# Retention scores of a fused three-layer kernel: three float32r products replaced by plain float32 products with two heads in the halves of the array's rows

## The chip, the cores and the metric

The kernel runs on one core of one Trainium2 chip. The metric is device time in microseconds for one launch; lower is better. Three runs of the kernel before gave 1452.89, 1457.00 and 1457.19 us, a median of 1457.0 us.

## The reference

Three layers follow one another. The first is retention over 8 batches, 8 heads, 576 positions and 64 features a head: scores, a causal decay mask, and a product with v. Its output, 4608 rows of 512, goes through a mixture of 8 experts with one expert for each row, and then through a dense layer with a squared rectifier.

```
scores = scale * np.matmul(q, k.transpose(0, 1, 3, 2))
ret = scores * Dmat[None, :, :, :]
attn = np.matmul(ret, v)                     # 8 x 8 x 576 x 64
logits = x @ w_gate;  expert_idx = np.argmax(logits, axis=1)
xe = x[mask];  h = np.maximum(xe @ w1[e], 0.0);  ye = h @ w2[e]
out[mask] = gate_w[mask, None] * ye          # for each of 8 experts
h = x @ w_in;  r = np.maximum(h, 0.0);  out = (r * r) @ w_out
```

## The kernel before

The work runs in three stages, one after the other: retention with the routing of the rows to experts, the experts, and the dense layer. The change touches only the first.

The 4608 rows are 36 tiles of 128. A tile's input, `in`, is 1 MB: q and k with their features on the partitions, v and k with their tokens on the partitions. In the array of partitions of q and k, partitions 0 to 63 hold one head of a pair and 64 to 127 the other, so that four blocks of 128 columns hold the eight heads. Five buffers hold `in`.

A loop over t, written out by hand in `body`, sets the order of work on each engine; each engine takes its instructions in that order. In round t it does the following.

- SyncE's queue starts the load of tile t+4 (L291), which needs the buffer of tile t-1, and then writes the rows of tile t-1 to DRAM in four transfers (L406).
- `scores(t + 1)`: TensorE multiplies k by q into two PSUM tiles `sc`, out of a ring of three. VectorE multiplies each by the mask into `r` (L343).
- `scale_v(t + 2)`: GpSimd scales v into `vs` (L316).
- `out_x(t)`: TensorE multiplies q by the running state (L385; for every ninth tile, which holds the ends of two batches, L378 with `zq`, a copy of q with zeros), and adds the product of `r` and `vs` (L389). VectorE scales the sum into `x` (L397) and transposes it in blocks into `xr` (L399).
- `state(t)`: TensorE adds k times v to the state (L361), and ScalarE copies it out into `sts` (L368).
- On every second tile there are router logits (L417, L421, L426, L427), and between t = 11 and the end one routing step at the end of a round, mostly on VectorE (L449 to L508, L162 to L191).
- In rounds 14, 20, 26 and 32 the first expert's weights are split into two float32r parts, by ScalarE (L99) and VectorE (L100).

A float32 product can be had from float32r products by splitting each operand into a high part, rounded to float32r, and the rest. `split(t + 3)` does that for k and q: ScalarE rounds k into `kh` (L299) and the two halves of q into `qh` (L302); GpSimd subtracts to get `kl` (L303), and VectorE and GpSimd subtract to get the two halves of `ql` (L306; one half each when t > 6, both on VectorE before). The tiles `qh` and `ql` (`qb` in the trace) hold each pair of heads side by side in 256 columns, with zeros in the other head's partitions, so one product over all 128 partitions gives the scores of two heads. `scores` then takes three such products for each pair: high by high, high by low, low by high (L338 to L340), 12 matmuls of 256 columns for a tile. The first two tiles, t < `EASY`, skip the split and use plain float32 operands straight from `in`, one head in partitions 0 to 63 and one in 64 to 127 (L330), 8 matmuls of 128 columns for a tile; each stands as two matmul records in the trace.

For t up to 6, `split(t + 3)` stands after `state(t)`; later it stands before `out_x(t)`.

Of the kernel before, what the change touches and what calls it, by code (L numbers as in the profile page):

```python
# [27 lines left out]
EASY = 2  # L28
BUSY = 6
# [10 lines left out]
def body(ctx, tc, att, tab_v, tab_x, masks, wg, ident, pick, cst, wu, wd, out):  # L40
# [70 lines left out]
    # ---- float64 weights: sign, exponent and 20 bits of the mantissa come from the high word, the  # L111
    # other 32 bits from the low word; kept in DRAM as two float32r parts ----
# [44 lines left out]
    def route(rt, t0, t1, ri, bank, inv, ct):  # L157
        """Adds, for the tokens of tiles t0 to t1 whose place among their expert's is ri, their numbers at their
        slots: the slot within a tile picks the row, expert and tile pick the column."""
# [58 lines left out]
    # a row of x_d and y_d keeps its features in the order (32-row quadrant, 128-feature chunk, 32)  # L218
    x_q = x_d.rearrange("n (a c) -> (n a) c", a=4)

    # (expert 0 has its first matrix's rows in that order too, so its rows need no reordering)
# [26 lines left out]
    # ================= retention, logits and routing =================  # L248
# [5 lines left out]
    with ExitStack() as es:  # L254
# [17 lines left out]
        qb = [[tabs.tile([128, 4, 2, 128], F32R, name=f"qb{i}{s}") for s in range(2)] for i in range(3)]  # L272

        in_t, vs_t, k_t, r_t, st_acc, xp_t = {}, {}, {}, {}, {}, {}
# [18 lines left out]
        def split(t):  # L293
            q = in_t[t][:, 0].rearrange("p (h n) -> p h n", h=4)
            k = in_t[t][:, 1]
            qh, ql = qb[t % 3]
            kh = sp_p.tile([128, 512], F32R, tag="kh", name="kh")
            kl = sp_p.tile([128, 512], F32R, tag="kl", name="kl")
            act.activation(out=kh, in_=k, func=AF.Copy)  # L299
            for s in range(2):  # L300
                o = slice(64 * s, 64 * s + 64)
                act.activation(out=qh[o, :, s], in_=q[o], func=AF.Copy)  # L302
            (pool if t > EASY else vec).tensor_tensor(out=kl, in0=k, in1=kh.bitcast(F32), op=ALU.subtract)  # L303
            for s in range(2):
                o = slice(64 * s, 64 * s + 64)
                (pool if s and t > BUSY else vec).tensor_tensor(  # L306
                    out=ql[o, :, s], in0=q[o], in1=qh[o, :, s].bitcast(F32), op=ALU.subtract
                )
            k_t[t] = kh, kl
            if kind(t)[1] == 4:  # L310
                act.activation(out=zq[:, :, 0], in_=q[:, :, 0:64], func=AF.Copy)
                act.activation(out=zq[:, :, 2], in_=q[:, :, 64:128], func=AF.Copy)
# [9 lines left out]
        def scores(t):  # L322
            m = msk[:, 1 if kind(t)[1] == 4 else 0]
            sc = [sc_ps.tile([128, 4, 128], F32, tag="sc", name="sc") for _ in range(2)]
            for p in range(4):
                cs = slice(128 * p, 128 * p + 128)
                if t < EASY:
                    for s in range(2):
                        o = slice(64 * s, 64 * s + 64)
                        pe.matmul(  # L330
                            sc[s][:, p], in_t[t][o, 1, cs], in_t[t][o, 0, cs],
                            start=True, stop=True, skip_group_check=True,
                        )
                    continue
                qh, ql = [a[:, p].rearrange("p s n -> p (s n)") for a in qb[t % 3]]
                kh, kl = [a[:, cs] for a in k_t[t]]
                o = sc[p // 2][:, 2 * (p % 2):2 * (p % 2) + 2].rearrange("p s n -> p (s n)")
                pe.matmul(o, kh, qh, start=True, stop=False, skip_group_check=True)  # L338
                pe.matmul(o, kh, ql, start=False, stop=False, skip_group_check=True)
                pe.matmul(o, kl, qh, start=False, stop=True, skip_group_check=True)  # L340
            for i in range(2):
                r = r_p.tile([128, 4, 128], F32, tag=f"r{i}", name=f"r{i}")
                vec.tensor_tensor(  # L343
                    out=r, in0=sc[i], in1=m.unsqueeze(1).to_broadcast([128, 4, 128]), op=ALU.mult
                )
                r_t[t, i] = r
# [23 lines left out]
        def out_x(t):  # L370
# [15 lines left out]
            for p in range(4):  # L386
                for s in range(2):
                    h = 2 * p + s
                    pe.matmul(  # L389
                        ps[64 * s:64 * s + 64, p], vs_t[t][:, 64 * h:64 * h + 64],  # L390
                        r_t[t, s][:, p] if t < EASY else r_t[t, p // 2][:, 2 * (p % 2) + s],
                        start=(c == 0 and p == 0), stop=(p == 3), skip_group_check=True,
                    )
# [125 lines left out]
        # The first LEAD tiles of expert 0's slots are kept for the tokens of the first three groups: those that  # L519
        # come later take no place below 128 * LEAD, so these tiles are known while the rest is still on its way.  # L520
# [40 lines left out]
        # the tensor engine's clock rises after some microseconds of work: it gets some while the first tiles load  # L561
# [20 lines left out]
        for i in (0, 1, 2):  # L582
            for a in qb[i]:
                pool.memset(a[0:64, :, 1].bitcast(F32), 0.0)
                pool.memset(a[64:128, :, 0].bitcast(F32), 0.0)
# [3 lines left out]
        if EASY < 3:  # L589
            split(2)  # L590
        fold = None
        for t in range(NT):
# [29 lines left out]
            if BUSY < t < NT - 3:  # L622
                split(t + 3)
# [4 lines left out]
            if t <= BUSY:  # L628
                split(t + 3)
# [4 lines left out]
            if t % 6 == 2 and 12 <= t < 36:  # L634
                w_q[t // 6 - 2] = split_unit(t // 6 - 2, raw.pop(t - 2), vec)
# [9 lines left out]
    # ================= experts =================  # L645
# [11 lines left out]
    # A token's place among its expert's is at most its number: tile i of an expert's slots holds no token of  # L657
    # the first i tiles.
# [33 lines left out]
    with ExitStack() as es:  # L692
# [40 lines left out]
        # the first 128 * LEAD slots of expert 0 are one part, the others are the other  # L733
# [55 lines left out]
        # ---- tokens beyond an expert's slots: 128 more of every expert in each round, as many rounds as the  # L789
        # fullest expert needs ----  # L790
# [158 lines left out]
    # ================= dense layer =================  # L949
# [100 lines left out]
def _tokens(a):  # L1050
    """[B, H, S, D] to [tile, token, feature]; tile 8 of every nine holds the last 64 tokens of two batches."""
    import numpy as np

    a = a.transpose(0, 2, 1, 3).reshape(4, 2, 576, 512)
    whole = a[:, :, :512].reshape(4, 8, 128, 512)
    last = a[:, :, 512:].reshape(4, 1, 128, 512)
    return np.concatenate([whole, last], 1).reshape(NT, 128, 512)
# [67 lines left out]
```

## Time and profile before

| | us |
|---|---|
| median of three runs | 1457.0 |
| lowest, highest run | 1452.89, 1457.19 |
| span of the profiled execution | 1541.4 |
| of it retention and routing, 0 to 202 | 202 |
| of it experts, 202 to 750 | 548 |
| of it dense layer, 750 to the end | 791 |

The page gives one time for the profiled execution, its span from the first to the last instruction; it is longer than the runs without a profile. Busy times are shares of such a span. A matmul's busy time includes its way through the array, which overlaps the next matmul, so the start of one block of matmuls minus the start of the block before it is the better measure of what a block costs TensorE. PEclk is the granted TensorE clock: 1.00 is 2.4 GHz, 0.50 is 1.2 GHz.

### The profile page before, as it was taken

Reading aid. Unit: us, or ns where it says so; the run is one execution under the profiler, and the core shown is the slowest. Engines: PE = TensorE matmul, PEld = TensorE weight load, DVE = VectorE, ACT = ScalarE, POOL = GpSimd, SP = SyncE. Lnnn points to the kernel's source line nnn. Section 1 sums busy time; section 2 is a strip of 40 time slices with the busy share of each in tenths; the row PEclk is TensorE's granted clock in tenths of the full one; section 3 lists DMA queues with packets and bytes.
Section 4 is the critical chain, followed back from the end, with each engine's and each line's share of the span. In section 5 each row is a group of like instructions: output and inputs, shape, how many; then the busy total and the mean of one; then the engine's idle time right before and its main releaser. Section 6 shows DMA issues by size and latency. Waiting matters only on the chain.

```text
span 1541.4 us, 20420 instructions
## 1 busy us (share of the span) xinstructions
PE 1445.4 (94%) x8081; PEld 1229.0 (80%) x8081; DVE 769.3 (50%) x1231; ACT 496.3 (32%) x866; POOL 397.0 (26%) x347
## 2 busy tenths in 40 slices
PE   7989899886979798789999999999999999999998
PEld 6878788685968687679888888888888888888887
DVE  7898965584848486574333333323232333323222
ACT  4555524242424243233222222222222222222222
POOL 5877736726354454711100000000000000000000
PEclk9999999988989899889999999999999999999999
DMA  8887634654546364634560202020200202020000
GB/s 308 277 265 251 206 115 141 217 166 150 187 142 218 117 223 144 197 110 183 162 252 5 51 0 55 1 55 1 55 1 1 55 1 55 1 55 0 28 0 28
DMA packets 92407, 172.51 MB, mean 112 GB/s; under 512 B 16654, under 2 KB 54030, under 8 KB 86672
## 3 DMA queue, kind: packets, MB, share of 16 engines
q1 hardware_dynamic: 82944, 151.03, 31.1%
q0 software_dynamic: 9360, 20.10, 4.1%
q8 instruction: 65, 1.06, 0.3%
q14 instruction: 38, 0.31, 0.1%
HBM read 125.86 MB, written 46.28 MB: 112 GB/s over the span
## 4 chain that ended last, share of the span: by engine, by line
PE 59%; issue 4%; DMA 1%; DVE 1%; POOL 0%; SPq 0%; ACT 0%; POOLq 0%; DVEq 0%
PE fl L971 25%; PE fa L994 8%; PE fa L993 8%; PE fa L992 8%; PE l L746 2%; PE l L747 2%; PE l L748 2%; PE acc L772 1%; PE acc L771 1%; PE acc L770 1%; DMA w<-wd_d 1%; DMA y_d<-y,sidx 0%; POOL y_d L229 0%; SPq L667 0%; DVE w L100 0%
## 5 line engine op out<-in xcount | busy, mean ns | idle before, releaser
L971 PE MATMUL fl<-xt,w 128*128 128x512 f32 (+1 forms) x1776 | 416.9, 384 | 1.8 <-DMA w<-wd_d 1.8
L971 PEld LDWEIGHTS fl<-xt,w 128*128 128x128 f32 x1776 | 328.1, 189 | 68.2 <-issue 2.2
L978 DVE TENSOR_TENSOR fr<-fr 128x512 f32<-128x512 f32 x144 | 99.9, 694 | 402.9 <-ACT fr L976 402.9
L992 PE MATMUL fa<-w,gh 128*128 128x512 f32 x576 | 224.1, 389 | 0.0
L993 PE MATMUL fa<-w,gh 128*128 128x512 f32 x576 | 224.1, 389 | 0.0
L994 PE MATMUL fa<-w,gl 128*128 128x512 f32 x576 | 224.1, 389 | 0.0
L976 ACT ACTIVATE fr<-fl 128x512 f32<-128x512 f32 x144 | 86.2, 599 | 417.6 <-PE fl L971 417.6
L746 PE MATMUL l<-xt,w 128*128 128x320 f32 (+1 forms) x480 | 154.9, 323 | 35.5 <-issue 17.5
L748 PE MATMUL l<-xt,w 128*128 128x320 f32 (+1 forms) x480 | 154.2, 321 | 11.0 <-issue 10.7
L747 PE MATMUL l<-xt,w 128*128 128x320 f32 (+1 forms) x480 | 154.5, 322 | 8.5 <-issue 8.4
L208 POOL DMA_INDIRECT xs<-x_d,qidx x140 | 151.0, 1078 | 44.3 <-issue 42.4
L982 DVE TENSOR_TENSOR gl<-fr,gh 128x512 fp32r<-128x512 f32 x144 | 99.7, 692 | 100.5 <-ACT gh L980 100.5
L772 PE MATMUL acc<-w,hl 128*128 128x512 f32 x320 | 127.4, 398 | 4.1 <-issue 3.7
L771 PE MATMUL acc<-w,hh 128*128 128x512 f32 x320 | 128.7, 402 | 2.3 <-issue 1.9
L770 PE MATMUL acc<-w,hh 128*128 128x512 f32 x320 | 128.9, 403 | 1.8 <-issue 1.8
L746 PEld LDWEIGHTS l<-xt,w 128*128 128x128 f32 x480 | 93.7, 195 | 45.3 <-issue 38.9
L980 ACT ACTIVATE gh<-fr 128x512 fp32r<-128x512 f32 x144 | 91.0, 632 | 109.8 <-DVE fr L978 109.8
L993 PEld LDWEIGHTS fa<-w,gh 128*128 128x128 f32 x576 | 108.2, 188 | 22.5
L992 PEld LDWEIGHTS fa<-w,gh 128*128 128x128 f32 x576 | 108.1, 188 | 22.5
L994 PEld LDWEIGHTS fa<-w,gl 128*128 128x128 f32 x576 | 108.0, 188 | 22.3
L753 DVE SCALAR_TENSOR_TENSOR hl<-l,hh 128x320 fp32r<-128x320 f32 (+2 forms) x128 | 59.9, 486 | 118.9 <-ACT hh L752 60.3
L747 PEld LDWEIGHTS l<-xt,w 128*128 128x128 f32 x480 | 94.0, 196 | 13.9 <-issue 11.4
(154 smaller groups left out, 1895.5 us busy)
## 6 DMA issues: line engine op xcount, KB each, us to landing
raw<-wu SPq DMA_DIRECT2D x62, 512.0 KB
in<-att SPq DMA_DIRECT2D x28, 1024.0 KB
craw<-wd SPq DMA_DIRECT2D x32, 512.0 KB
wd_d<-cw SPq DMA_DIRECT2D x32, 512.0 KB
w<-wd_d SPq DMA_DIRECT2D x16, 1024.0 KB
x_d<-xr SPq DMA_DIRECT2D x144, 64.0 KB
yi<-y_d SPq DMA_DIRECT2D x32, 256.0 KB
out<-fo SPq DMA_DIRECT2D x32, 256.0 KB
```

Source lines behind the costliest of these rows:

```text
L208: pool.indirect_dma_start(out=xs, out_offset=None, in_=src, in_offset=bass.IndirectOffsetOnAxis(ap=index, axis=0),)
L746: pe.matmul(ps, w[:, 0, k], hi[:, k, cs], start=(k == 0), stop=False)
L747: pe.matmul(ps, w[:, 0, k], lo[:, k, cs], start=False, stop=False)
L748: pe.matmul(ps, w[:, 1, k], hi[:, k, cs], start=False, stop=(k == 3))
L770: pe.matmul(acc[i], hh[:, cs], w[:, 0], start=(f == 0), stop=False)
L771: pe.matmul(acc[i], hh[:, cs], w[:, 1], start=False, stop=False)
L772: pe.matmul(acc[i], hl[:, cs], w[:, 0], start=False, stop=(f == 7))
L971: pe.matmul(ps, w[:, s, k], x[:, k, ts], start=(n == 0), stop=(n == 11))
L978: vec.tensor_tensor(out=gg, in0=r, in1=r, op=ALU.mult)
L992: pe.matmul(acc[i], gh[:, cs], w[:, 0], start=(f == 0), stop=False)
L993: pe.matmul(acc[i], gh[:, cs], w[:, 1], start=False, stop=False)
L994: pe.matmul(acc[i], gl[:, cs], w[:, 0], start=False, stop=(f == 15))
```

## The change

All tiles now take the form that tiles 0 and 1 had: `scores` is 8 float32 matmuls of 128 columns with 64 rows of the array each, the two heads of a pair in its lower and upper rows, written to two PSUM tiles in turn. `split` goes, and with it `kh`, `kl`, `qh`, `ql`, their zeroing on GpSimd and their buffers; what is left of it is the copy into `zq` for every ninth tile, `spread_q(t + 3)`, which stands before `out_x(t)` for all t. The order of heads in `r` changes with it. The subtraction that splits the first expert's weights moves from VectorE to GpSimd.

```diff
-EASY = 2
-BUSY = 6
...
-        qb = [[tabs.tile([128, 4, 2, 128], F32R, name=f"qb{i}{s}") for s in range(2)] for i in range(3)]
...
-        def split(t):
-            q = in_t[t][:, 0].rearrange("p (h n) -> p h n", h=4)
-            k = in_t[t][:, 1]
-            qh, ql = qb[t % 3]
-            kh = sp_p.tile([128, 512], F32R, tag="kh", name="kh")
-            kl = sp_p.tile([128, 512], F32R, tag="kl", name="kl")
-            act.activation(out=kh, in_=k, func=AF.Copy)
-            for s in range(2):
-                o = slice(64 * s, 64 * s + 64)
-                act.activation(out=qh[o, :, s], in_=q[o], func=AF.Copy)
-            (pool if t > EASY else vec).tensor_tensor(out=kl, in0=k, in1=kh.bitcast(F32), op=ALU.subtract)
-            for s in range(2):
-                o = slice(64 * s, 64 * s + 64)
-                (pool if s and t > BUSY else vec).tensor_tensor(
-                    out=ql[o, :, s], in0=q[o], in1=qh[o, :, s].bitcast(F32), op=ALU.subtract
-                )
-            k_t[t] = kh, kl
+        def spread_q(t):
             if kind(t)[1] == 4:
+                q = in_t[t][:, 0].rearrange("p (h n) -> p h n", h=4)
                 act.activation(out=zq[:, :, 0], in_=q[:, :, 0:64], func=AF.Copy)
                 act.activation(out=zq[:, :, 2], in_=q[:, :, 64:128], func=AF.Copy)
...
-                if t < EASY:
-                    for s in range(2):
...
-                    continue
-                qh, ql = [a[:, p].rearrange("p s n -> p (s n)") for a in qb[t % 3]]
-                kh, kl = [a[:, cs] for a in k_t[t]]
-                o = sc[p // 2][:, 2 * (p % 2):2 * (p % 2) + 2].rearrange("p s n -> p (s n)")
-                pe.matmul(o, kh, qh, start=True, stop=False, skip_group_check=True)
-                pe.matmul(o, kh, ql, start=False, stop=False, skip_group_check=True)
-                pe.matmul(o, kl, qh, start=False, stop=True, skip_group_check=True)
+                for s in range(2):
+                    o = slice(64 * s, 64 * s + 64)
+                    pe.matmul(
+                        sc[s][:, p], in_t[t][o, 1, cs], in_t[t][o, 0, cs],
+                        start=True, stop=True, skip_group_check=True,
+                    )
...
-                        r_t[t, s][:, p] if t < EASY else r_t[t, p // 2][:, 2 * (p % 2) + s],
+                        r_t[t, s][:, p],
...
-        for i in (0, 1, 2):
-            for a in qb[i]:
-                pool.memset(a[0:64, :, 1].bitcast(F32), 0.0)
-                pool.memset(a[64:128, :, 0].bitcast(F32), 0.0)
...
-        if EASY < 3:
-            split(2)
...
-            if BUSY < t < NT - 3:
-                split(t + 3)
+            if t + 3 < NT:
+                spread_q(t + 3)
             out_x(t)
             state(t)
...
-            if t <= BUSY:
-                split(t + 3)
...
-                w_q[t // 6 - 2] = split_unit(t // 6 - 2, raw.pop(t - 2), vec)
+                w_q[t // 6 - 2] = split_unit(t // 6 - 2, raw.pop(t - 2), pool)
```

The line numbers of the changed kernel are lower by 26 in this part: L343 becomes L317, L397 L371, L399 L373, L427 L401, L361 L335, L385 L359, L389 L363, L417 L391, L368 L342, L421 L395; L330 becomes L311.

VectorE's queue before, from the masking of tile 15 (`r`) to that of tile 16, in round 14: `qb` is a half of the low part of q for tile 17, `lgt` a logits reduction, `w` the weights of the first expert.

```order
L343 TENSOR_TENSOR r_1175<-sc,msk 128x512
L343 TENSOR_TENSOR r_1177<-sc,msk 128x512
L427 TENSOR_REDUCE lgt<-lg 128x16
L306 TENSOR_TENSOR qb_151<-in,qb_150 64x4x128
L397 TENSOR_TENSOR x<-x,tabx 128x4x128
L399 STREAM_TRANSPOSE xr<-x 128x4x4x32
L100 TENSOR_TENSOR w<-raw,w 128x1024
L343 TENSOR_TENSOR r_1252<-sc,msk 128x512
```

The same place in VectorE's queue of the changed kernel:

```order
L317 TENSOR_TENSOR r_981<-sc,msk 128x512
L317 TENSOR_TENSOR r_983<-sc,msk 128x512
L401 TENSOR_REDUCE lgt<-lg 128x16
L371 TENSOR_TENSOR x<-x,tabx 128x4x128
L373 STREAM_TRANSPOSE xr<-x 128x4x4x32
L317 TENSOR_TENSOR r_1046<-sc,msk 128x512
```

The subtraction for tile 17, which stood ahead of the scaling of tile 14, is gone, and so is the subtraction for the weights. What is left works on tiles 14, 15 and 16.

ScalarE's queue before, in rounds 8 to 10: `kh` and `qb` are the high parts of k and q, `ls` the logits and `sts` the copy of the state.

```order
L299 ACTIVATE kh<-in 128x512
L302 ACTIVATE qb_146<-in 64x4x128 x2
L421 ACTIVATE ls<-lg 128x256
L299 ACTIVATE kh<-in 128x512
L302 ACTIVATE qb_148<-in 64x4x128 x2
L368 ACTIVATE sts_145<-stp 64x4x64 x2
```

ScalarE's queue of the changed kernel, where `zq` is spread for tile 8 and in the rounds after it:

```order
L293 ACTIVATE zq<-in 128x4x64
L294 ACTIVATE zq<-in 128x4x64
L342 ACTIVATE sts_143<-stp 64x4x64 x2
L342 ACTIVATE sts_142<-stp 64x4x64 x2
L395 ACTIVATE ls<-lg 128x256
L342 ACTIVATE sts_145<-stp 64x4x64 x2
```

Every copy of the state stood behind the rounding of a tile that is three rounds ahead. Now only the spreading of every ninth tile stands there.

TensorE's queue before, the end of the 12 score matmuls of tile 4 and what follows them in round 3:

```order
L340 MATMUL sc<-qb_148,kl 128x256
L338 MATMUL sc<-qb_148,kh 128x256
L339 MATMUL sc<-qb_149,kh 128x256
L340 MATMUL sc<-qb_148,kl 128x256
L417 MATMUL lg<-x,wg_139 32x256 x4
L385 MATMUL x<-in,sts_142 128x128 x4
L389 MATMUL x<-r_362,vs 64x128 x4
L389 MATMUL x<-r_364,vs 64x128 x4
L361 MATMUL stp<-vs,in 64x64 x8
```

The same place in TensorE's queue of the changed kernel, with all score matmuls of tile 4:

```order
L311 MATMUL sc<-in 128x128 x8
L391 MATMUL lg<-x,wg_139 32x256 x4
L359 MATMUL x<-in,sts_142 128x128 x4
L363 MATMUL x<-r_312,vs 64x128
L363 MATMUL x<-r_314,vs 64x128
```

The 12 matmuls became 8, whose operands come from `in` alone; the order around them is as it was.

## Rows read from the trace of the kernel before

**Rows 1.** Busy time by stage: each engine's busy us (instructions), granted clock, DMA share, GB/s.

```profile
0.00:202.00 202.00, 175.56 (x2033) 152.77 (x2034) 176.62 (x286) 100.49 (x198) 141.27 (x116) 0.94 0.79 252
202.00:750.00 548.00, 484.26 (x2550) 424.63 (x2549) 336.95 (x569) 188.06 (x327) 254.76 (x230) 0.93 0.50 165
750.00:1541.00 791.00, 785.60 (x3502) 651.56 (x3500) 255.73 (x377) 207.74 (x342) 0.98 (x1) 1.00 0.14 40
```

**Rows 2.** The same view of stretches within the first stage; PE, PEld, DVE, ACT, POOL.

```profile
10.00:22.00 12.00, 8.53 (x86) 7.91 (x84) 9.20 (x11) 4.31 (x8) 5.24 (x4) 0.72 1.03 404
40.00:60.00 20.00, 19.53 (x245) 17.12 (x244) 14.77 (x22) 10.88 (x22) 14.70 (x12) 1.00 0.92 281
100.00:120.00 20.00, 19.12 (x236) 17.01 (x239) 18.11 (x32) 10.47 (x22) 16.16 (x13) 1.00 0.93 293
120.00:140.00 20.00, 16.34 (x189) 14.31 (x191) 19.73 (x30) 11.99 (x24) 15.92 (x12) 0.91 0.70 213
```

**Rows 3.** Instruction groups of 0 to 203 us: busy, mean ns | idle before, releasers.

```profile
L343 DVE TENSOR_TENSOR r<-sc,msk 128x512 f32<-128x512 f32 x72 | 45.8, 676 | 2.4 <-PE sc L330 2.2
L303 POOL TENSOR_TENSOR kl<-in,kh 128x512 fp32r<-128x512 f32 x33 | 44.3, 1343 | 32.4 <-ACT kh L299 32.4
L306 DVE TENSOR_TENSOR qb<-in,qb 64x512 fp32r<-64x512 f32 x39 | 43.1, 1105 | 12.2 <-ACT qb L302 12.1
L399 DVE STREAM_TRANSPOSE xr<-x 128x512 f32<-128x512 f32 x36 | 25.6, 712 | 1.2
L397 DVE TENSOR_TENSOR x<-x,tabx 128x512 f32<-128x512 f32 x36 | 24.4, 677 | 1.5 <-PE x L389 1.5
L299 ACT ACTIVATE kh<-in 128x512 fp32r<-128x512 f32 x34 | 21.4, 631 | 41.5 <-DMA in<-att 41.2
L100 DVE TENSOR_TENSOR w<-raw,w 128x1024 fp32r<-128x1024 f32 x4 | 5.9, 1478 | 0.0
```

**Rows 4.** Timeline from 49 to 60 us: a load's issue, and round 8 behind it.

```profile
49.12 0.35 SPq L291 DMA_DIRECT2D in<-att  x1
...
57.18 0.63 ACT L299 ACTIVATE kh<-in 128x512 fp32r<-128x512 f32 x1 [2.92 <-DMA in<-att]
...
58.36 1.35 DVE L306 TENSOR_TENSOR qb<-in,qb 64x512 fp32r<-64x512 f32 x1 [1.43 <-ACT qb L302]
...
59.64 0.67 DVE L397 TENSOR_TENSOR x<-x,tabx 128x512 f32<-128x512 f32 x1
```

**Rows 5.** TensorE's timeline at the start: the scores of tile 1, then the next block.

```profile
8.93 1.16 PE L330 MATMUL sc<-in 64*128 64x128 f32 x16 [2.64 <-DMA in<-att]
10.02 1.09 PE L389 MATMUL x<-r,vs 128*64 128x128 f32 x16
```

**Rows 6.** TensorE's timeline from 41 to 43.5 us: first of 12 score matmuls, then L426.

```profile
41.49 0.39 PE L338 MATMUL sc<-qb,kh 128*128 128x256 f32 x1
...
43.03 0.38 PE L426 MATMUL lg<-idn,ls 128*128 128x128 f32 x2
43.25 1.06 PE L385 MATMUL x<-in,sts 128*128 128x128 f32 x8
```

**Rows 7.** TensorE's timeline from 119.9 to 123.1 us: one round's other blocks, clock 1.00.

```profile
119.92 0.64 PE L417 MATMUL lg<-x,wg 128*32 128x256 f32 x8
120.48 1.16 PE L385 MATMUL x<-in,sts 128*128 128x128 f32 x8
121.57 1.09 PE L389 MATMUL x<-r,vs 128*64 128x128 f32 x16
122.50 0.63 PE L361 MATMUL stp<-vs,in 128*64 128x64 f32 x16
123.06 0.39 PE L338 MATMUL sc<-qb,kh 128*128 128x256 f32 x1
```

**Rows 8.** TensorE's timeline at the lower clock, 128 to 130 us.

```profile
128.13 1.98 PE L389 MATMUL x<-r,vs 128*64 128x128 f32 x16
129.89 0.96 PE L361 MATMUL stp<-vs,in 128*64 128x64 f32 x16
```

More of the change, by code (lines that the diff above doesn't have):

```diff
@@ L271, in body @@
         sts = [tabs.tile([128, 4, 128], F32, name=f"sts{i}") for i in range(4)]
-        qb = [[tabs.tile([128, 4, 2, 128], F32R, name=f"qb{i}{s}") for s in range(2)] for i in range(3)]
-        in_t, vs_t, k_t, r_t, st_acc, xp_t = {}, {}, {}, {}, {}, {}
+        in_t, vs_t, r_t, st_acc, xp_t = {}, {}, {}, {}, {}
         lead_s = []
@@ L326, in scores @@
                 cs = slice(128 * p, 128 * p + 128)
-                if t < EASY:
-                    for s in range(2):
[L329 to L333, printed above, removed]
-                    continue
-                qh, ql = [a[:, p].rearrange("p s n -> p (s n)") for a in qb[t % 3]]
-                kh, kl = [a[:, cs] for a in k_t[t]]
-                o = sc[p // 2][:, 2 * (p % 2):2 * (p % 2) + 2].rearrange("p s n -> p (s n)")
-                pe.matmul(o, kh, qh, start=True, stop=False, skip_group_check=True)
-                pe.matmul(o, kh, ql, start=False, stop=False, skip_group_check=True)
-                pe.matmul(o, kl, qh, start=False, stop=True, skip_group_check=True)
+                for s in range(2):
[4 more added lines that the diff above has]
+                    )
             for i in range(2):
```

## The prediction

> **What bounds the kernel now.** I read the busy time by stage first. The three stages follow one another, and the change touches the first, which ends at about 202 us [rows 1]. In the dense stage TensorE is busy for 785.6 of 791 us, so a gain made before it has nothing to hide behind there; in the expert stage it is busy for 484 of 548. In the first stage no engine is full on the average: TensorE 175.6, VectorE 176.6, GpSimd 141.3, ScalarE 100.5 of 202 us, the DMA engines at a share of 0.79.
>
> The stretches of that stage come second [rows 2]. They show that the limit changes. From 120 to 140 us VectorE is busy for 19.73 of 20 us. From 40 to 60 us it is busy for 14.77 only, while the DMA share is 0.92 at the full clock.
>
> The groups of instructions come third, since they name what each waits for [rows 3]. VectorE spends 43.1 us on the low parts of q, 39 instructions at a mean of 1105 ns, though the masking of a tile twice as large takes 676. Before them it stands idle for another 12.2 us, nearly all of it waiting for ScalarE's rounding of q; ScalarE in turn stands idle for 41.5 us ahead of the rounding of k, waiting for the load.
>
> The timeline of one round shows how these join into a loop [rows 4]. The load of tile 11 is issued at 49.12 us in round 7. ScalarE, after 2.92 us of waiting for it, rounds k at 57.18, which is 8.06 us after the issue. VectorE waits 1.43 us for the rounding and subtracts at 58.36, and only behind that, at 59.64, comes the scaling of tile 8, which had nothing to do with tile 11. So in most rounds a load has to land within about two rounds, not for the scores of its tile, which come two rounds later, but because the split stands in front of other work in two strict queues. The stage lasts 202 us / 36 = 5.6 us a tile.
>
> **The change, part by part.**
>
> *TensorE's scores.* Before: 12 matmuls from 41.49 to 43.03, so 1.54 us a tile at the full clock [rows 6]. After: the form that tiles 0 and 1 have already. Tile 1's block starts at 8.93 and the next block at 10.02, so 1.09 us at most, also at the full clock [rows 5]. Over 34 tiles that is 34 x 0.45 = 15 us less on TensorE. The eight matmuls in the halves of the rows must run partly at once: 8 x 128 columns in 1.09 us is 136 ns each, whereas the four full-row float32 matmuls of L385 take 1.09 us too, 273 ns each [rows 7].
>
> The Trainium skill has a rule that speaks against this part: "FP8 and Floating Point Precision", section "TensorE Precision Notes", says that true float32 makes four passes through the array. By it alone, 8 x 128 columns in four passes are 4096 columns against 12 x 256 = 3072, and TensorE would lose by the change. The trace differs: the block of 8 is the shorter one. What it would cost if the halves did not overlap is a rival below.
>
> *VectorE.* The 43.1 us of L306 go, and so do the 5.9 us of the four weight splits [rows 3]; of its 176.6 us some 127.6 are left. Of these 45.8 + 25.6 + 24.4 = 95.8 us are masking, transposing and scaling, or 2.66 us a tile; the other 31.8 are routing, logits and the start. The 12.2 us of idle time before L306 go too.
>
> *ScalarE and the loads.* All of `kh` and `qh` go, and with them the wait of 41.2 us. The first readers of a load are now GpSimd's scaling two rounds after the issue's round, and the scores three rounds after it. At about 4 us a round that is 12 us for a landing that took 8.06. What is late next is `zq`: for four tiles ScalarE waits for a load issued a round earlier and the copy of the state stands behind it. Two rounds of 4 us just cover 8.06 us; I take 2 us for the four, and with no cover at all they would cost 4 x 4 = 16.
>
> *GpSimd.* It loses `kl` and its half of `ql` and gets four weight subtractions of 128 x 1024. By `kl`, 1343 ns for half the size [rows 3], they take 2.7 us each. Behind each stands the scaling of v for a tile that is multiplied rounds later. I cost them at nothing; uncovered, 4 x 2.7 = 11 us. The zeroing of `qb` at the start goes, and the first scaling of v may start sooner; the wait for tile 1, up to 8.93 us, hides that. At the lowest it costs nothing, and it can gain nothing while that load is late.
>
> *The ring of `sc`.* Scores now write both PSUM tiles from their second matmul on, so they wait for the masking of the tile before one half block earlier than they did, and masking can start only near the end of the block. Before, the first PSUM tile was whole after six of the twelve. VectorE has 2.66 us of work in a round of some 4, so I price this at nothing in an ordinary round, and at up to 0.5 us (half a block of 1.09) in each of 36, 18 us, if VectorE were always on the path.
>
> *The sum for the stage.* TensorE's own order by the starts of blocks [rows 5 to 7]: scores 36 x 1.09, products with the state 32 x 1.09 (24 tiles, and twice for four more), L389 36 x 0.93, L361 32 x 0.56, logits 17 x 0.56 and their turning 17 x 0.22. That is 39.2 + 34.9 + 33.5 + 17.9 + 9.5 + 3.7 = 138.7 us. Tile 0's scores lie ahead of 8.93 us, so the stage cannot end before 8.93 + 138.7 - 1.09 = 146.5. VectorE's floor is lower: 127.6.
>
> To 146.5 come four terms. First the lower clock: a mean of 0.94 in the stage [rows 1] means that 12% of it, 24 us, ran at 1.2 GHz. There L389 took 129.89 - 128.13 = 1.76 us [rows 8] against 0.93, so about 24 x 0.47 = 11 us were lost; I keep them. Second the routing: in a group of six rounds VectorE has 6 x 2.66 + 31.8 / 4 = 24 us and TensorE six times 138.7 / 36, or 23; an estimate of 1 us a group, 4 in all. Third the small routing matmuls and the turning of rows that I left out, an estimate of 5 from the same 0.22 us for two turns. Fourth `zq`, 2. That makes 168.5. Loads that are not quite steady I allow 3.5 for, and take an end at 172 us, 30 us sooner.
>
> The profiled span is 1541.4 us, and it is all that the page gives of that execution; the median of the runs is 1457.0, or 0.945 of it. I scale the gain alike: 30 x 0.945 = 28, and 1457 - 28 gives 1429 us.
>
> **Rivals.**
>
> *The transfers become the bound.* The stage moves 252 GB/s x 202 us = 50.9 MB. The busiest steady stretch moved 293 GB/s at a share of 0.93 [rows 2]; at that rate it takes 174 us, and the last three tiles' work, 12 us, follows: 186, a gain of 16 x 0.945 = 15 and 1442 us. For it speaks the share of 0.92. Against it speak the 404 GB/s of the first loads, several of which were under way at once, as they will be when loads no longer have to land within two rounds.
>
> *No overlap of the halves.* If each matmul of half the rows took what one with all rows takes, the 273 ns of L385, the block would last 2.18 us, 1.09 more than I counted: 36 x 1.09 = 39, an end at 211 and 1457 + 9 x 0.945 = 1466. Rows 5 speak against it, unless tile 1 is not like the others. The Trainium skill's rule of four passes, named above, is the same case; by it, at 2.4 GHz, the block would be an estimate of 8 x 0.213 = 1.7 us, and the time about 1450.
>
> *Slower: the clock.* If blocks of half-filled rows let the clock fall, the stage is set by TensorE at 1.2 GHz. With half of its 138.7 us there, at 1.76 / 0.93 = 1.9 times the time, 62 us come on top of 172: 234, 32 us later than now and 1487 us. The point from which it decides is 30 / 0.9 = 33 us of matmuls more at the lower clock, a quarter of the stage. Against it: the stage ran at 1.00 from 40 to 60 us and from 100 to 120, where TensorE was busiest, and at 0.91 or less where it waited [rows 2]; after the change it waits less.
>
> *The gain is lost in the expert stage.* It ran at a clock of 0.93 with 64 us of idle TensorE [rows 1]. If that idle time were set by transfers or the routing's tail rather than by the end of retention, an earlier start would only wait longer: 1457. Its weights are loaded one unit after the other as units are used, which speaks against it.
>
> **How the numbers follow.** My forecast has 0.64, the transfers 0.21, no overlap 0.04, the clock 0.05, and no gain at the end 0.06. A difference of 0.3%, some 4 us, is about what a measurement of this kernel can tell from none; faster by more than that are the first two, so 0.85 for faster, 0.06 for the same and 0.04 + 0.05 = 0.09 for slower. Below, the range goes to TensorE's floor with no allowance but the small matmuls, 146.5 + 5: a gain of 50 x 0.945 = 48 and 1409, say 1410. Above, it takes in the transfers, 1442, and with them half of the 14 us that `zq` can still cost, which makes 1449. The likeliest case alone lies between 1418 and 1438.
>
> **What would show it.** In the profile after, the first matmuls of the experts should start near 172 us. The score block should take 1.1 us from its start to the next block's where nothing waits. VectorE should be busy for about 128 us of the stage with no group above 800 ns at 128 x 512, ScalarE should have no long waits for `in` but at `zq`, and TensorE should be the busiest engine, with 85% or more. A DMA share of 0.93 or more with TensorE waiting for `in` would show the first rival; a block of 1.7 us or more the second; a mean clock under 0.85 in the stage the third; a stage end at 172 with an unchanged total the fourth. I am wrong in the mechanism if rounds still last over 5 us in stretches without routing.

## The result

The changed kernel ran in 1430.38 us (median of four runs, 1428.15 to 1436.04), the kernel before beside it in 1455.56 (1452.89 to 1457.19): a ratio of 0.9847 with an interval of [0.9824, 0.987], 25.2 us faster. A second set gave 1434.6 against 1453.63: 0.9865 [0.9833, 0.9897], 19.0 us. The forecast was 1429 us.

In some sets of runs the expert stage of every version took up to 113 us longer (572 us against 459; it was 548 in the profile of before [rows 1]), and one chip had sets of both kinds, so that the kernel before has medians of 1569.3, 1538.82 and 1451 to 1456, and below only ratios to runs of the same set and the ends of the first stage are compared. The profiled execution of after is the slowest of its four, 1436.04 us.

The profile after, busy time by stage with the columns of [rows 1]:

```profile
0.00:183.00 183.00, 155.39 (x2170) 131.67 (x2171) 119.90 (x242) 40.03 (x96) 50.38 (x46) 0.95 0.87 278
183.00:642.00 459.00, 449.05 (x2535) 407.53 (x2535) 334.97 (x566) 186.07 (x324) 261.33 (x230) 0.99 0.60 195
642.00:1434.00 792.00, 786.82 (x3516) 653.03 (x3514) 257.65 (x381) 209.24 (x344) 1.47 (x2) 1.00 0.14 40
```

VectorE fell from 176.6 to 119.9 us, ScalarE from 100.5 to 40.0, GpSimd from 141.3 to 50.4, TensorE from 175.6 to 155.4; the DMA share rose from 0.79 to 0.87. The dense stage is as it was. The last scaling of `x` marks the end of the first stage: 201.8 us in before, 182.8 now, 19.0 sooner. The stretches that answer to [rows 2], and one more:

```profile
40.00:60.00 20.00, 19.08 (x284) 16.81 (x284) 11.94 (x23) 4.38 (x12) 4.37 (x5) 1.00 0.98 320
100.00:120.00 20.00, 20.00 (x313) 17.15 (x314) 18.27 (x39) 6.00 (x14) 8.73 (x6) 1.00 0.95 302
120.00:140.00 20.00, 16.73 (x252) 14.38 (x249) 13.34 (x24) 5.47 (x13) 6.54 (x5) 1.00 0.94 299
160.00:180.00 20.00, 13.66 (x175) 11.74 (x171) 9.58 (x24) 5.91 (x13) 5.86 (x5) 0.83 0.50 150
```

The DMA engines are at 0.94 to 0.98 in the first three of these stretches; from 100 to 120 us TensorE has no idle time either. From 160 to 180 us the DMA share is 0.50, since the last load lands at 167.4 us, and TensorE is busy for only 13.66 us at a granted clock of 0.83: something stops the loop there. The groups of 0 to 184 us name it (columns of [rows 3]), and the last row stands where ScalarE's wait of 41.5 us stood:

```profile
L359 PE MATMUL x<-in,sts 128*128 128x128 f32 x192 | 28.7, 296 | 13.6 <-ACT sts L342 13.6
L98 POOL TENSOR_TENSOR w<-raw,w 128x1024 fp32r<-128x1024 f32 x4 | 10.2, 2547 | 21.0 <-ACT w L97 14.4 <-DMA x_d<-xr 6.6
L293 ACT ACTIVATE zq<-in 128x256 f32<-128x256 f32 x4 | 1.7, 416 | 28.8 <-DMA in<-att 28.8
```

Four spreadings of `zq` wait for 28.8 us of loads, and TensorE waits 13.6 us for the copy of the state queued behind them. The timeline shows the two worst of the four, each between two scalings of `x`, and ahead of the first the issue of the load that it waits for:

```profile
73.48 0.51 SPq L92 DMA_DIRECT2D raw<-wu  x1
74.09 0.66 SPq L288 DMA_DIRECT2D in<-att  x1
...
75.89 0.68 DVE L371 TENSOR_TENSOR x<-x,tabx 128x512 f32<-128x512 f32 x1
...
82.24 0.42 ACT L293 ACTIVATE zq<-in 128x256 f32<-128x256 f32 x1 [10.36 <-DMA in<-att]
...
83.81 2.08 PE L359 MATMUL x<-in,sts 128*128 128x128 f32 x8 [4.85 <-ACT sts L342]
...
87.84 0.69 DVE L371 TENSOR_TENSOR x<-x,tabx 128x512 f32<-128x512 f32 x1 [6.51 <-PE x L363]
...
160.45 0.69 DVE L371 TENSOR_TENSOR x<-x,tabx 128x512 f32<-128x512 f32 x1
...
167.38 0.42 ACT L293 ACTIVATE zq<-in 128x256 f32<-128x256 f32 x1 [10.88 <-DMA in<-att]
...
168.11 0.77 ACT L342 ACTIVATE sts<-stp 64x256 f32<-64x256 f32 x2
...
168.93 2.08 PE L359 MATMUL x<-in,sts 128*128 128x128 f32 x8 [5.53 <-ACT sts L342]
...
172.96 0.69 DVE L371 TENSOR_TENSOR x<-x,tabx 128x512 f32<-128x512 f32 x1 [7.51 <-PE x L363]
```

Between 87.84 and 160.45 us lie 17 tiles, 4.27 us each. The two steps with a spreading, 75.89 to 87.84 and 160.45 to 172.96, took 11.95 and 12.51 us, some 8 us more each. The load that the first one waits for was issued at 74.09, behind a transfer of weights and only 1.80 us ahead of the scaling at 75.89, and landed 8.15 us later, as `zq` starts at 82.24. Behind both stops L359 ran at half the clock (2.08 us, against 1.06 in [rows 6]), which is a part of the 8 us. The score block came out as forecast:

```profile
43.22 1.16 PE L311 MATMUL sc<-in 64*128 64x128 f32 x16
44.31 0.64 PE L391 MATMUL lg<-x,wg 128*32 128x256 f32 x8
```

44.31 - 43.22 = 1.09 us at the full clock, where [rows 6] had 1.54.

### The profile page after: what moved, and what is told of

It reads as the page before. It is cut to its first block, busy times and chain, and to the rows that moved or that the text cites. A ratio compares the mean times of both kernels' runs of the same rounds, so it can differ in the third digit from the quotient of the medians.

```text
span 1434.2 us, 20323 instructions
## 1 busy us (share of the span) xinstructions
PE 1391.3 (97%) x8217; PEld 1192.2 (83%) x8217; DVE 712.5 (50%) x1187; ACT 435.3 (30%) x764; POOL 313.2 (22%) x277
## 4 chain that ended last, share of the span: by engine, by line
PE 72%; issue 3%; DMA 1%; POOL 0%; SPq 0%; ACT 0%; POOLq 0%; DVE 0%
PE fl L937 27%; PE fa L959 9%; PE fa L958 9%; PE fa L960 9%; PE l L712 3%; PE l L713 3%; PE l L714 3%; PE acc L737 3%; PE acc L736 3%; PE acc L738 3%; DMA w<-wd_d 1%; DMA y_d<-y,sidx 0%; POOL y_d L227 0%; SPq L633 0%; DMA yi<-y_d 0%
## 5 line engine op out<-in xcount | busy, mean ns | idle before, releaser
L206 POOL DMA_INDIRECT xs<-x_d,qidx x140 | 154.0, 1100 | 44.4 <-issue 42.4
L712 PE MATMUL l<-xt,w 128*128 128x320 f32 (+1 forms) x480 | 150.2, 313 | 8.8 <-DVEq L759 6.2
L713 PE MATMUL l<-xt,w 128*128 128x320 f32 (+1 forms) x480 | 149.8, 312 | 0.0
L714 PE MATMUL l<-xt,w 128*128 128x320 f32 (+1 forms) x480 | 149.7, 312 | 0.0
L960 PEld LDWEIGHTS fa<-w,gl 128*128 128x128 f32 x576 | 108.0, 188 | 22.4
L736 PE MATMUL acc<-w,hh 128*128 128x512 f32 x320 | 125.7, 393 | 0.0
L737 PE MATMUL acc<-w,hh 128*128 128x512 f32 x320 | 125.3, 392 | 0.0
L712 PEld LDWEIGHTS l<-xt,w 128*128 128x128 f32 x480 | 90.7, 189 | 12.1 <-issue 6.6
L713 PEld LDWEIGHTS l<-xt,w 128*128 128x128 f32 x480 | 90.7, 189 | 2.4 <-DVE xt L689 0.2
L714 PEld LDWEIGHTS l<-xt,w 128*128 128x128 f32 x480 | 90.7, 189 | 0.0
```

Of the source, the lines that this page charges most:

```text
L206: pool.indirect_dma_start(out=xs, out_offset=None, in_=src, in_offset=bass.IndirectOffsetOnAxis(ap=index, axis=0),)
L712: pe.matmul(ps, w[:, 0, k], hi[:, k, cs], start=(k == 0), stop=False)
L713: pe.matmul(ps, w[:, 0, k], lo[:, k, cs], start=False, stop=False)
L714: pe.matmul(ps, w[:, 1, k], hi[:, k, cs], start=False, stop=(k == 3))
L736: pe.matmul(acc[i], hh[:, cs], w[:, 0], start=(f == 0), stop=False)
L737: pe.matmul(acc[i], hh[:, cs], w[:, 1], start=False, stop=False)
```

## The experiments

Three questions: what had held the old kernel (a wait in VectorE's queue, VectorE's work, or TensorE's), what holds the new one (transfers or a wait), and what `zq` costs. First, the old kernel again, for the level of the spans.

> The kernel before, unchanged, profiled once more. Its first profile spans 1541 us against runs of 1456, with 548 us in the expert stage, where the changed kernel's profile has 459. Theory A: the extra 85 us are a matter of that one profiled execution, and a second profile spans 1450 to 1460 with the first stage ending at 200 to 203 us and the expert stage at 460 to 470. Theory B: the profile of this kernel always adds them, and the span is above 1520 again. Under A the gain of the change, 25 us, is 19 us from the first stage and 6 from elsewhere.

1563.4 us beside runs of the same kernel at 1569.3; the first stage ended at 200.2 and the expert stage took 572 us. Theory A fell, and of B only the span came: the runs beside this profile were as long.

```profile
200.00:772.00 572.00, 488.88 (x2548) 425.59 (x2548) 336.50 (x570) 188.45 (x326) 251.45 (x230) 0.90 0.48 158
```

The long expert stage comes without the change too; what brings it stays open. The first stage ends where it did (201.8 in the first profile).

**Was it the wait in front of VectorE's work?** Edit of before (e6): the split a round later, so its load has had time to land.

```diff
-            if BUSY < t < NT - 3:
-                split(t + 3)
+            if 0 < t < NT - 2:
+                split(t + 2)
...
-            if t <= BUSY:
-                split(t + 3)
```

> The kernel before with all its float32r splits, but split(t + 2) instead of split(t + 3) in front of out_x(t) in every round, so that it reads a load a round older. Theory A, the split cost time because it made VectorE and ScalarE wait for a load three tiles ahead: the first stage ends at 180 to 188 us instead of 200 to 202, and the ratio to the kernel before is 0.985 to 0.992. Theory B, the work itself on VectorE (176 us of it) sets the stage: it ends at 196 us or later, and the ratio is above 0.995.

1466.8 us, ratio 1.0098 [1.0079, 1.0116], slower; stage end 210.4. The edit brought a wait of its own: TensorE now waits for GpSimd's half of the low part, 22.4 us.

```profile
PE sc L339 <- POOL qb L306: 22.4, 17, 2.2
```

So this run could not settle it. The next (e9) keeps the distance of three tiles and puts the split behind the work instead:

```diff
-            if BUSY < t < NT - 3:
-                split(t + 3)
             out_x(t)
             state(t)
...
-            if t <= BUSY:
+            if t < NT - 3:
                 split(t + 3)
```

> The kernel before with all its float32r splits and the same engines for them, but split(t + 3) stands behind state(t) in every round, as it does for t up to 6, instead of in front of out_x(t). The same work and the same three tiles of lead, but VectorE scales tile t and ScalarE copies the state before they meet a load. Theory A, what the split cost was the place of its waits in the two queues: the first stage ends at 182 to 190 us and the ratio is 0.983 to 0.993. Theory B, the splits' work on three engines sets the stage wherever it stands: it ends at 197 us or later and the ratio is 0.996 or more.

1454.81 us, ratio 1.0021 [1.0003, 1.0039]; stage end 202.0. ScalarE's wait for loads, 41.2 us in before [rows 3], fell to 11.5, and the end stayed:

```profile
ACT kh L299 <- DMA in<-att: 11.5, 3, 10.1
```

And the opposite (e11): the changed kernel with a wait for the same load put back at the same place in VectorE's queue, with next to no work (a copy of one column).

```diff
+            if t + 3 < NT:
+                seen = sp_p.tile([128, 1], F32, tag="seen", name="seen")
+                vec.tensor_copy(seen, in_t[t + 3][:, 1, 0:1])
             out_x(t)
```

> The changed kernel with one copy of 128 x 1 on VectorE in front of each out_x(t) that reads the input of tile t+3, so that VectorE waits for that load as it did in the split, with next to none of its work. Theory A, the place of the wait was the cost: the first stage ends at 195 to 202 us and the gain shrinks to 0 to 8 us. Theory B, the work was the cost: the stage ends within 5 us of 185 and the time stays at 1430 to 1437.

1433.35 us, ratio 0.9866 [0.9827, 0.9905]; stage end 182.0. The stage of e9, that of e11, and VectorE's wait in e11 (us in all, times, longest):

```profile
0.00:202.00 202.00, 174.60 (x2032) 151.42 (x2033) 179.24 (x285) 100.57 (x198) 140.37 (x116) 0.95 0.78 252
```

```profile
0.00:182.00 182.00, 160.81 (x2168) 135.83 (x2169) 118.85 (x274) 40.14 (x96) 49.22 (x46) 0.95 0.87 280
```

```profile
DVE seen L594 <- DMA in<-att: 43.0, 24, 5.2
```

With the split's work the stage ends at 201.8 (in front) or 202.0 (behind); without it at 182.8 (no wait) or 182.0 (VectorE waiting 43.0 us for loads). In neither kernel does the place of the wait move the end; the work does. For the old kernel that rests on e9: in e11 the stops at `zq` shrank to 18.0 us of waiting (28.8 in after), so a new wait partly took the place of another one for the same loads.

**Whose work?** VectorE's (e7): two subtractions of half a tile each round, put back into the changed kernel in front of `out_x`.

```diff
+            for s in range(2):
+                o = slice(64 * s, 64 * s + 64)
+                extra = sp_p.tile([128, 512], F32, tag="extra", name="extra")
+                vec.tensor_tensor(out=extra[o], in0=in_t[t][o, 1], in1=in_t[t][o, 0], op=ALU.subtract)
             out_x(t)
```

> The changed kernel with 72 subtractions of 64 x 512 on VectorE that nobody reads, two in front of each out_x(t), from the tile already in use; near 48 us at 0.67 us each. Theory A, transfers and the waits at zq set the stage, and VectorE had 60 us of slack in it: the stage ends at 180 to 190 us. Theory B, VectorE's 43 us of subtraction were the cost of the split: the stage ends at 196 us or later.

1453.8 us beside 1453.63 for before; stage end 194.6.

```profile
0.00:195.00 195.00, 166.86 (x2187) 141.80 (x2188) 177.66 (x314) 40.13 (x96) 51.92 (x46) 0.94 0.82 261
```

```profile
L595 DVE TENSOR_TENSOR extra<-in 64x512 f32<-64x512 f32 x72 | 57.5, 798 | 0.5
```

VectorE is as busy as it was before the change (177.7 us), with no rounding or subtraction of k and q on ScalarE or GpSimd, and 8 to 12 us of the stage's gain are gone (from 182.8, or 186.9 in the second run of the changed kernel), though the stops at `zq` shrank here too, to 17.1 us of waiting. The end lies between the two theories, 190 and 196. The total of this one run lost all of the gain, the stage not: 1257.0 us lay behind it (1451.6 - 194.6), 4 to 8 more than in other versions (below), and no run shows why.

TensorE's (e8): the same eight score matmuls, but four in one half of the rows and then four in the other.

```diff
-            for p in range(4):
-                cs = slice(128 * p, 128 * p + 128)
-                for s in range(2):
+            for s in range(2):
+                for p in range(4):
+                    cs = slice(128 * p, 128 * p + 128)
```

> The changed kernel with the four score matmuls of the lower rows first and the four of the upper rows after them, so that neighbours in the order no longer use different rows. Theory A, the block of 1.09 us is short because neighbours in different halves overlap: the block takes 1.7 to 2.2 us from its start to the next block's. Theory B, a matmul of 64 rows costs less whatever its neighbour does: 1.1 us again. In either case the first stage, which waits for transfers, moves by less than 36 x 1.1 us, to 183 to 200.

```profile
40.80 1.71 PE L311 MATMUL sc<-in 64*128 64x128 f32 x16
42.44 0.64 PE L391 MATMUL lg<-x,wg 128*32 128x256 f32 x8
```

The block takes 42.44 - 40.80 = 1.64 us in place of 1.09: the same matmuls are shorter when neighbours in the queue lie in different halves. That the halves then work at once fits this, but four neighbours of a half also write to one PSUM tile here, and no run parts the two. Yet the kernel took 1436.12 us beside 1434.6 for the changed one, and the stage ended at 183.0: 36 x 0.55 = 20 us more on TensorE did not move the end. At least 8 of them went into time that TensorE had spent waiting: the stops at `zq` fell to 19.2 us, and L359's wait for the state from 13.6 to 5.4.

**What holds the new stage?** The second run of the changed kernel (e5) came with these:

> The changed kernel, unchanged, once more. In the run of the four kernels before this one, the kernel before took 1569 us where it had taken 1456, with the difference in the expert stage. Theory A: the gain lies in the first stage and does not depend on that; the ratio is 0.982 to 0.988 and the first stage ends at 178 to 184 us, whatever the level of the times. Theory B: what the expert stage loses differs between the two kernels, and the ratio lies outside 0.98 to 0.99 though the first stage ends at 178 to 184.

Its stage ended at 186.9, later than the 178 to 184 that both theories had, with 32.9 us of waiting at `zq`. Then less to move (e3): three quarters of each load from tile 4 on; the state's product reads another part of the tile in place of the last quarter, which is left out.

```diff
-            n = 3 if kind(t)[1] == 4 else 4
+            n = 3
...
-                        acc[64 * h:64 * h + 64, p], in_t[t][:, 3, cs], vs_t[t][:, cs],
+                        acc[64 * h:64 * h + 64, p], in_t[t][:, 1, cs], vs_t[t][:, cs],
```

> The changed kernel, but of tiles 4 to 35 the last quarter of the input (k by tokens, 0.25 MB a tile) is not loaded, and the state is made from k by features in its place; the output and the routing are other than the reference's, so only the first stage is compared. 28 tiles load 0.25 MB less (the other four never loaded it), 7 MB or 14% of the stage's 51 MB. Theory A, transfers set the pace: at 300 GB/s the stage ends 15 to 24 us sooner, at 160 to 168. Theory B, TensorE's order and zq set it: no more than 5 us sooner, 178 or later.

1520.8 us beside 1569.3, and the first stage, with ScalarE's wait at `zq`:

```profile
0.00:164.00 164.00, 150.39 (x2170) 128.19 (x2171) 118.29 (x242) 40.00 (x96) 50.48 (x46) 0.98 0.85 266
```

```profile
ACT zq L293 <- DMA in<-att: 14.9, 3, 8.4
```

266 GB/s x 164 us = 43.6 MB in place of 50.9, 14% less, and an end at 163.8, 19 to 23 us sooner. A part of that are shorter stops, 14.9 us of waiting after 28.8; but e2 and e10 below have no stops and all the bytes, and end 10 to 14 us later than this run, so the bytes themselves are on the path. Loads issued two rounds earlier, with seven buffers (e4):

```diff
-        in_p = scope(es, "in_p", 5)
+        in_p = scope(es, "in_p", 7)
...
-            if t + 4 < NT:
-                load(t + 4)
+            for v in (4, 5, 6) if t == 0 else (t + 6,):
+                if v < NT:
+                    load(v)
```

> The changed kernel with 7 input buffers instead of 5 and loads issued two rounds earlier (tile t+6 in round t). Theory A, the rate of the transfers sets the pace: the stage ends within 5 us of 183, and the time is 1425 to 1432. Theory B, the landing time of a load (7.9 us) sets it, at zq and at the scores: waits for the input disappear, the stage ends near 167 and the time is 1413 to 1420.

1546.93 us, ratio 0.9876 [0.9804, 0.9949]; stage end 182.8. The wait at `zq` all but went; others, queued behind the earlier loads, came in its place, so this run alone decides nothing.

```profile
DVE x L371 <- DMA tabx<-tab_x: 12.6, 2, 11.7
ACT w L97 <- DMA raw<-wu: 12.5, 3, 8.5
ACT zq L293 <- DMA in<-att: 1.5, 1, 1.5
```

**What does `zq` cost?** The spreading two rounds later (e2, and again beside e9 and e11 as e10):

```diff
-            if t + 3 < NT:
-                spread_q(t + 3)
+            if t + 1 < NT:
+                spread_q(t + 1)
```

> The changed kernel with the spreading of zq for tile t+1 instead of t+3 in round t, so that it reads a load that has landed long ago. Theory A, ScalarE's waits at zq cost what TensorE shows behind them (13.6 us in four waits, and a lower clock after two of them): the first stage ends 12 to 18 us sooner, near 167, and the time is 1413 to 1420. Theory B, the loads set the pace (0.95 of the DMA engines, 300 GB/s) and zq's waits only take the slack: the stage ends 0 to 5 us sooner and the time is 1425 to 1430.

> The changed kernel with zq spread for tile t+1 in round t, once more, since its first run had no run of the changed kernel beside it at the same level of times. There its first stage ended at 174 us against 183 and 187 in two profiles of the changed kernel. Theory A: 9 to 13 us carry to the end, 1421 to 1427 where the changed kernel takes 1430 to 1435, a ratio to the kernel before of 0.976 to 0.982. Theory B: they are lost in the expert stage, and the ratio is 0.984 to 0.988 as for the changed kernel.

1544.05 us against 1569.3, 0.986 [0.9788, 0.9933], stage end 174.0; and 1424.4 against 1451.2, 0.9808 [0.9769, 0.9847], stage end 177.3. That beats the changed kernel by 5.5 to 13 us at the end of the stage, between the two theories of e2 (12 to 18, and 0 to 5). At the end of the kernel the intervals of both runs overlap those of the changed kernel. In e10, its stage, two of the longest waits, and the step that took 11.95 us in after:

```profile
0.00:177.00 177.00, 149.61 (x2166) 126.39 (x2166) 115.89 (x241) 39.74 (x96) 49.10 (x46) 0.99 0.91 288
```

```profile
DVE xr L373 <- DMA x_d<-xr: 27.4, 22, 3.6
PE sc L311 <- DMA in<-att: 21.9, 20, 3.2
```

```profile
75.25 0.68 DVE L371 TENSOR_TENSOR x<-x,tabx 128x512 f32<-128x512 f32 x1
80.98 0.69 DVE L371 TENSOR_TENSOR x<-x,tabx 128x512 f32<-128x512 f32 x1 [1.14 <-PE x L363]
```

The step shrank to 5.73 us and the wait at `zq` is gone, but the tiles between 80.98 and 162.64 us now take 4.80 us each, where they took 4.27, as if the stops had let the transfers catch up. TensorE waited for loads 20 times. To see whether that is the landing of single loads or their rate, the last run has both edits, the spreading two rounds later and loads up to two rounds earlier, brought in by steps (e12):

```diff
-        in_p = scope(es, "in_p", 5)
+        in_p = scope(es, "in_p", 7)
...
-            if t + 4 < NT:
-                load(t + 4)
+            for v in range(4, min(NT, t + 5 + (t >= 6) + (t >= 8))):
+                if v not in in_t:
+                    load(v)
...
-            if t + 3 < NT:
-                spread_q(t + 3)
+            if t + 1 < NT:
+                spread_q(t + 1)
```

> The load's values for the expert scores are again converted two rounds later, and besides the load of a later round is issued up to two rounds earlier (seven buffers in place of five). Theory A, the rate of the transfers (about 290 to 300 GB/s while they run) sets the pace of the first stage: its end stays at 172 to 178 us and the ratio lies within 0.004 of the 0.981 of the version with five buffers. Theory B, the time at which one load lands still costs the 21.9 us that TensorE waited for loads there: the stage ends near 160 us and the ratio is 0.975 or less.

1522.91 us against 1538.82, 0.9899 [0.9816, 0.9981]; stage end 179.2.

```profile
0.00:179.00 179.00, 156.96 (x2167) 132.77 (x2168) 121.62 (x241) 39.63 (x96) 50.51 (x46) 0.96 0.88 285
```

```profile
PE sc L311 <- DMA in<-att: 4.2, 3, 2.5
DVE xr L373 <- DMA x_d<-xr: 27.0, 18, 3.8
```

TensorE's wait for loads fell from 21.9 to 4.2 us and the stage did not get shorter. VectorE's wait of 27.0 us for the rows to be written out is not what took its place, since e10 has it too (27.4). What rose is TensorE's busy time, from 149.6 us at a granted clock of 0.99 to 157.0 at 0.96. So earlier loads did not help, at the same 285 to 288 GB/s; that the rate is the reason, this run alone does not show. Neither theory came as it stood: the end of 179.2 lies above A's 172 to 178 and far from B's 160, and the ratio is a little worse than A allowed, though its interval reaches e10's.

## Why the prediction was right, and where not

*The time.* 1429 was forecast and 1430.4 and 1434.6 came. The stage went as forecast in kind and less far in size, 13 to 19 us sooner (182.8 or 186.9 after 200.2 or 201.8) in place of 30. That the total came within 1.4 us all the same was in part luck: the scaling below took 2 us off the forecast gain, and of the 25.2 us of the first set the profiled stage ends account for 19.0. Where the other 6 come from stays open.

*That a gain in the first stage reaches the end.* Right, within some 4 us. What the profiled spans hold behind the first stage is 1249.1 us in e9 (1451.1 - 202.0), 1249.8 in e10 (1427.1 - 177.3), 1251.4 in after (1434.2 - 182.8) and 1253.4 in e5 (1440.3 - 186.9), and only e7, with 1257.0, lies further off. The rival that loses it in the expert stage is out.

*The scaling by 0.945.* Wrong. A profiled span is not longer than the run as such (1434.2 of 1436.04 us in after). That of before was longer by its expert stage; its first stage was not stretched (201.8, against 200.2 and 202.0 in e1 and e9). The gain in the stage should have been carried over as it stood; with it the forecast would have been 1457 - 30 = 1427.

*"These join into a loop": the split stands in front of other work in two strict queues.* This step fell. e9 moves the split behind and gains nothing; e11 puts a wait of 43.0 us back and loses nothing. VectorE's 176.6 us in a stage of 202 were the heavier half: on its own (e7, one run) work of that size brings the end to 194.6, and all of the split's work together to 202.0. Whose the last 7.4 us are, the roundings on ScalarE or the subtractions on GpSimd and the waits between the three, stays open; no run had one of them alone. The term "The 43.1 us of L306 go, and so do the 5.9" was in the prediction only as a floor of 127.6 (measured 119.9); it was the larger source of the gain.

*TensorE's scores.* The size was exact, 1.09 us, and worth nothing: e8 gives 20 us of it back and the stage ends where it did. TensorE's order, on which the sum of 168.5 us was built, does not set the end of the new stage. The Trainium skill's rule of four passes ("FP8 and Floating Point Precision", "TensorE Precision Notes"), an estimate of 1.7 us for the block, agrees with e8's 1.64; with the halves in turn the trace has 1.09, and there it decides.

*`zq`, "I take 2 us for the four, and with no cover at all they would cost 16".* The mis-sized term. Rounds were 4.27 us and the landing 8.15, both as assumed (4 and 8.06). The failure is in when the load was issued: at the end of its round, 1.80 us ahead of the next scaling, and not at its start, so it had little more than one round of cover instead of two. Two of the four stops, those with a transfer of weights just ahead of the load, lengthened their steps by 8 us each. Taking the stops away gave 5.5 to 13 us, not 16: TensorE then waited 21.9 us for loads (e10).

*The transfers, rival at 0.21.* Its stage end, 186, was met (182.8 and 186.9), by a different sum: stops at `zq` on top of a pace that the transfers set. Its rate of 293 GB/s is near that of the three stretches above (299 to 320), e3 shows the bytes on the path, and in e12 earlier loads did not help. The forecast of "loads that are not quite steady", 3.5 us, should have been this rival's floor of 174, where e2 and e10 ended (174.0, 177.3).

*The clock and "no overlap".* Both out: the granted clock rose from 0.94 to 0.95, and the block took 1.09 us.

*GpSimd's weights at nothing.* Borne out: 2.55 us each, near the 2.7 taken, and GpSimd, busy for 50.4 of 183 us, had the room.

*The ring of `sc` at nothing.* Borne out: in after TensorE waited 0.5 us in all for the masking, and the masking 6.0 us for scores.

## What to carry to other kernels

A wait shown ahead of an instruction on a nearly full engine is not yet a cost: ask whether the engine's work without the wait fills the stage, and move the wait alone before blaming it. When engines become free, compute first what the stage's bytes take at the best steady rate in its own trace, here 50.9 MB at 293 GB/s, and take that as the floor; then look for the one reader left that comes too soon behind its load's issue. A profiled span that is longer than the runs has to be compared stage by stage before a gain is scaled by it.

## What the runs showed of the hardware

Eight float32 matmuls of 128 columns on 64 rows took 1.09 us with the halves of the rows in turn and 1.64 us with four in one half and then four in the other: order in the queue alone is worth a third.

The subtraction of 64 x 512 on VectorE took 1105 ns on the mean in before [rows 3] and 798 in e7, and the reason shows within each trace. In e7 (shortest, median and longest, in ns):

```profile
L595 DVE TENSOR_TENSOR extra<-in x72: 660/689/1564, 11.2 to 193.8; 64x512 f32<-64x512 f32 x72
```

The 44 of these 72 during which GpSimd ran no instruction took 660 to 690 ns, the other 28 took 987 on the mean. In before only 3 of the 39 on VectorE had no instruction of GpSimd beside them, and took 671 to 689 ns; the other 36 took 1141. So of the 43.1 us of L306 an estimate of 17, 39 x (1105 - 677) ns, was the price of GpSimd's work at the same time. The masking, which reads one of its inputs from PSUM, took 674 ns on the mean beside GpSimd and 685 without it in before. That fits the Trainium skill ("GPSIMD Engine Reference", "Specifications"), by which GpSimd shares its memory interface with VectorE's instructions that have two inputs in SBUF; no run here changed GpSimd's work alone.

And transfers of this mix, loads of 1 MB with 64 KB writes of rows between them, ran at 299 to 320 GB/s with a DMA share of 0.94 to 0.98 in three stretches of after.
